# U^T x in column quarters and V in four 32-row tiles: a change to the last three batches of a fused linear-attention and mixer kernel

## The chip, the cores and the metric

The kernel runs on one core of a Trainium2 chip. The metric is the device time of one execution in microseconds. A core has five engines with queues of their own: PE (TensorE, matmuls), ACT (ScalarE), DVE (VectorE), POOL (GpSimd) and SP (SyncE, which here only issues DMAs). Each works through its queue in order; semaphores tie them together. Matmul results land in PSUM, which has eight banks of 512 fp32 columns, and ACT or DVE move them from there to the on-chip memory (SBUF).

## The reference

Four batches of 768 steps. Gated linear attention with 8 heads of 48 gives x (768 x 384 per batch), and a mixer follows: a low-rank mix over the sequence (rank 32) and an MLP over the channels.

```
for t in range(S):
    state = alpha[:, :, t, :, None] * state + einsum('bhd,bhe->bhde', k[:, :, t], v[:, :, t])
    y[:, :, t] = einsum('bhd,bhde->bhe', q[:, :, t], state)
x = y as (batch, 768, 384)
u = x + (x^T @ U @ V)^T          # U: 768 x 32, V: 32 x 768
out = u + relu(u @ w_ch1) @ w_ch2   # w_ch1: 384 x 1536, w_ch2: 1536 x 384
```

## The kernel before

The sequence of a batch is cut into six chunks of 128 steps. Each chunk goes through a chain: the logarithm of alpha (ACT), cumulative sums (PE), exponentials (ACT), scaling of k and q (POOL or DVE), transposes of both (PE and a copy, or in batch 3 one transposing DMA per chunk, line 588, called from `QUEUE_T`), scores (PE, line 604 or 435), masks (DVE), a state update, the output y (PE, lines 666 and 671 or 508 and 518) and a copy of it into `xb`, which is x in bf16. In ten of the 24 chunks (`PAIRS`: three chunk pairs of batch 0, two of batch 1) the work is laid out in another way, with pairs of steps; these use 64-row tiles of the PE array, and their rows are called even and odd parts in U and V (`ue_sb`, `ve_sb` in place of `u_sb`, `vm_sb`).

`stage_mix` then does the low-rank mix of one batch:

- U^T x (`f_utx`, line 686): six matmuls, one per chunk, each with 32 columns of U as the weights and all 384 columns of x moving. Chunk c writes to partitions 32 (c mod 4) onwards of one bank, so the four column groups of the array work side by side, and the four groups of 32 partitions hold four partial sums. ACT or DVE copies them to `utx` (128 x 384).
- V's part (line 716): for each chunk one matmul with 128 rows. `ve_sb` and `vm_sb` hold V four times below each other, so the product adds up the four partial sums. Each takes a bank, and a DVE addition (line 717) makes `ub`, which is u in bf16, from it and `xb`.
- The transposes of u to `uT`, in pairs of chunks: by PE (line 736) and a copy in batches 1 and 2, by a transposing DMA (line 722) in batch 3 (`QUEUE_U`). Batch 0 makes `uT` directly by matmuls (lines 705, 708).

`mlp1` (line 767, called a first-MLP group when its three matmuls stand together) makes one 128-row block of the hidden layer for half the sequence, and ACT (line 777) or DVE (line 779) take the relu. `mlp2` (line 793, three groups of four matmuls for each chunk, called second-MLP groups) and a DVE addition (line 799) make the output, which goes out by DMA (lines 802, 804).

The order of all work is not made by loops. `Plan.add` only lists each group of instructions with the engines that may run it; the listed dependencies decide which PSUM banks and buffers are bound together. `Plan.run` then goes through a text, `TABLE`, three characters for each group: two say which group, one says on which engine it runs (P, A, D, G, S). `SLOTS` names the bank or buffer for each new tile. So the place of a group in its engine's queue is the order of the text, and an engine never passes over a group that waits. The numbers beside the engines in `P.add` (`mm(...)`, 385, 460 and so on) are a planner's costs; nothing at run time reads them.

```
    def run(self, table, slots):
        nxt = iter(slots)
        for n in range(0, len(table), 3):
            ...
            op = self.ops[CODE.index(table[n]) * len(CODE) + CODE.index(table[n + 1])]
            for b in op.bufs:
                if b.slot is None:
                    b.slot = b.pool.slots[CODE.index(next(nxt))]
            op.fn({"P": "PE", "A": "ACT", "D": "DVE", "G": "POOL", "S": "SP"}[table[n + 2]])
```

Input tiles (alpha, k, q, v and the weights) and output tiles share a pool of 40 buffers; SP issues all DMAs, loads, stores and transposes, from one queue.

Of the kernel before, what the change touches and what calls it, by code (L numbers as in the profile page):

```python
# [16 lines left out]
A8SCcABASCzABQSETACePChACfAA+SCgACjDC1PC4AC3AC2AEVPEYABISA9SCiDCkPCmDClPBBSC5GEXADjADlPDnAEWACnDDmACoPCqDA-SCdGCrPCsDBDS  # L17
C0GDCPBCSC6GC7PBESCvPCpDC8PC+DDKACtPCuDCwPCxDDDDC9AC-PDADDBDABSAFGAGPAHDAJPAKADMPDPABKSCyDDEPDNADGPDFDDqGDsPBJSDpGDrPDtA
DuDDHPDJADZPBYSG2ABSSEaGBHSDLGDoAEcPDyPEeADIDBFSDQGDaPDbDDSPDUDDvPDwDBMSBLSDkGDzPD0DDxDG4PD8AD+PBRSEZGEbPEdDD3PDcPDdDDOA
BGSDRGDTPDVDG5AEAAD1PD2DBUSGfABOSEDGEfPEhDEgDD-AG7ABNSECGEBAG6ABTSBcSEUABPSD9GGhPGiAGjAGkAD4PELPBVSBWSGlGGmGBgSBXSGgGAAS  # L20
ADGBZSG8GAiSAjGAQSAeSAfGAgSAhGDWPDXDEiPD5PD7ABkSD6AEjPEkDEFPEEPEHAHNADYDEGDElPEMPENDAOSAPGARGEmPDfPAMSANGDePEnPEoADgPDiD
DhAAYSAZGBaSG9GAWSAUSAVGEIPEJDEKDHmAHPPHSAEPPGnPAXGASSATGHQABdSHTGBbSG3GEpAHRABiSBfSHOGAaSBhSBeSBoSAcSAkSBlSBjSAmSBpSAoS
BqSBmSGoPGqDGpDEOPAqSBnSHoPHrAEQPESDAuSAsSGuPGvDGwDEqPGrPGtDGsDERAErPHpAHqAHtGE8PE5PAwSAySEwPG+PHADE2PBrSEsAExPEyAE6PE7D
FFPE9PE+DA2SE3PEtPEzPFBPFCDFHPEuPFJPFGDE4AEvAE0PE1AF1PH-AFIDGyPF5PF3PF4DE-PFADFfPFgDF6AF2AFDPFhPFiAGxDFlPFmAFdPA4SACSFED
A0SFKDFLPFMAFNPFODG-PFjPFkAFeDA6SFVPFWAIBPICAFRPFSAHUGHBDHCPHDDAdGBsSGzPIEAIDAHFPFtPHGDHHDHIGIGGG0AAbAFuAHVPHXAG1AFnPHJP
B0SBwSBySB4SB8SFPPBuSBzSFQAHEDHKPHLAHMAHcPHdDHeDHsDIFAIVAFTPFUAFoAFrPFsAFpPHvPFqDHfDHxAHWPIXPIYAHuPHwDFvPFwDFZPFaDFzPF0D
HYAHiPHZPHbDHaDIZAAnAHyPHzDIHDFbPApAFcAHhPFxPFyAFXPHjPHkAHlAFYAHnGH1PH2DH3DH4DIIPIKAH6PAlGIaGIcPIbGIdPIfAIJPArGGTPIeAH7P
GNPH0DH8PH+AILDIMPH9DIODIgPIhDGBPIAGIPPH5GIRDF7PGZPHgGAzGAtAAvAAxAGOPINDITPF8PIQDIiDISGIWAIjPA5GGaPA3AGCPIUAAEGIkAIlPImD
GUPA1GA7AGbPGcDIvPIwDALGIzPI0DI1PI2DF9PF+DItPIuDGDPKLAGPPInPIpPIqDGEDKNPK0AI3PIxPIyDIoDKfAKOAI4AKPAKhPKjAKnGGVPGWDK2PK3A
LJAKlAJfPJgALeAKRAIrPIsDJRPJjPJSAJkDJdPJeAKiAKkAK6AKQAI5PJHPJIDJPPJQAJLPJMAI-PJAAK5AK4ALgPLkAJFPJGDJJPJKDLjABxSKmGKoPKqA  # L30
JTPJUDI6DKTGKVPJnPJoDLiALhABvSKMGBtSKSGKgAKUPJXPKWDKXDKbPKcDJlPLLPLMAJYDJbPJmAB9SB2SK8GKvPJBPK+PKwDKxDLAACASJcDJDPJEAB1S
KpPKrDGQDLOAK7GLNAJCAI9PI+ALPACESK9PK-DCMSNlAI7PI8DJVPJWALzAB3SK1GKsPKuDLBPLDDLCDKYPKZDJvPJNPJOAB6SLRGLTPLVAJhPL1PL2AL3A
B+SCCSB5SLHPLIANnPNqAB-SKtDLfALlGLnPKaDJwPL5GLQDCBSL4GLEPNrAKyPKzAJiAOIAB7SLKALpAGHPJZPGIPLSPLUAJaALFDLGGLmGKBPL6PL8DGJP
L7PGKDL9ALoPLqACNSCISCFSNoANsGLZPLaDJxPJyDNpACGSNtGKCPCKSCLSCQSCUSCDSLWPLXDL+PLrPKdPKeALYDLtDKDPJ7PLuPN2AN4PN5AJ8PJpPLbG
LsDLvDL-DLwGMADL0GOaAOcPOgAOfAOdACHSNmGN3GLcPN6ALdAN+GJ9PLxPLyDKEDMBPJqPNuSNvPNwDMCAMDPJrPOeAGMSNxDJ+DMEAN7AN8AOKPOMAAIG
MTPMUDMNPJ1PMLPMRPKGPMODJsDMMDCSSCRSOhGNyPNzDN0PMHPMIDKHPMFPMGDOsAOuPKIPMPPMQAMSDMJPMKDOOAMVPMWDKJDJ2PCWSOvAOLAMfPMXPMYD
J3PMjPM7POiGCYSO+AGFSCTSGGSPAPN1AONAObGGYSCJSCXSOtGCaSGSSKFSGLSN9GOwACPSOjSCVSOzGO0DOPDMkDMgDOxAOyAPBAPCAMbPMcDMpPMqAMlP
MmAJ4DNBPODPNDPMZPM-POEDMaAM8ANCACOSOQGNADM1PM2AOkPM5PNEDMxPMyAN-SM9PMhPM3PM4AJuSF-SMtPM6AMuAOJGOVPCZSPDGPEDOmDOlDOFDOWD
OXGMdPMeDM+AOnPOoDOpGNFPNGDMnPMoAMvPMiAOqPOrAOAPOBDO1SO2PO3DO4DOCDORSJ-SOSPOUDNHPMrPMsANRPMzPO5PO6DO7GOTDO8PO9ANSPGRSCbS
O-APFSJ5SPGPM0DPIDPHDGXSOGPOHANTPNUDOYPMwANIPPJPPKAOZAGASNJPNbPPLPNMPNcPPMAPPPPQDPSPPXPPNPPODPRSPYDPTDNdPNKDPUPPVDPWSNWP  # L40
# [45 lines left out]
class Plan:  # L86

    warm = None
# [36 lines left out]
    def run(self, table, slots):  # L128
        nxt = iter(slots)
        for n in range(0, len(table), 3):  # L130
            if table[n : n + 2] == "++":
                for _ in range(CODE.index(table[n + 2])):
                    self.warm()
                continue
            op = self.ops[CODE.index(table[n]) * len(CODE) + CODE.index(table[n + 1])]
            for b in op.bufs:
                if b.slot is None:
                    b.slot = b.pool.slots[CODE.index(next(nxt))]
            op.fn({"P": "PE", "A": "ACT", "D": "DVE", "G": "POOL", "S": "SP"}[table[n + 2]])

# [6 lines left out]
def kernel(  # L147
# [14 lines left out]
    C = 128  # L162
# [20 lines left out]
    QUEUE_U = (3,)  # L183
    P = Plan()
# [13 lines left out]
    filler = h1_s[1][:, 0, 0:512]  # L198
# [66 lines left out]
    bank.free[7] = 28000.0  # L265
    P.warm = lambda: nc.tensor.matmul(ps[:, 7, :], lhsT=filler[:, 0:128], rhs=filler, start=True, stop=True)

# [55 lines left out]
    def paired(b, c):  # L323
        return c // 2 < PAIRS[b]
# [355 lines left out]
    def stage_mix(b, xb, ub, uT):  # L680
# [10 lines left out]
        if b == 0:  # L691
            P.add({"PE": mm(DM)}, lambda e: f_utx(range(0, 4)), r=[x for c in range(4) for x in xk(b, xb, c)] + ["ue"], w=[xu], mode="C")
            P.add({"PE": mm(DM)}, lambda e: f_utx(range(4, NC)), r=[x for c in range(4, NC) for x in xk(b, xb, c)] + ["ue"], w=[xu], mode="C")
        else:
            P.add({"PE": mm(DM, DM)}, lambda e: f_utx(range(NC)), r=[x for c in range(NC) for x in xk(b, xb, c)] + ["ue" if paired(b, c) else "u" for c in range(NC)], w=[xu], mode="C")
        utx = Buf(utxs)
        P.add({"ACT": 385, "DVE": 460}, lambda e: copy(e, utx(), xu()[:, 0:DM]), r=[xu], w=[utx])
        if b == 0:
# [15 lines left out]
        for c in range(NC):  # L714
            hb = Buf(bank)
            P.add({"PE": mm(DM)}, lambda e, c=c, hb=hb: nc.tensor.matmul(hb()[:, 0:DM], lhsT=(ve_sb if paired(b, c) else vm_sb)[:, c * C : (c + 1) * C], rhs=utx(), start=True, stop=True), r=[utx, ("ve" if paired(b, c) else "vm", c // NT)], w=[hb])  # L716
            P.add({"DVE": 465}, lambda e, c=c, hb=hb: nc.vector.tensor_tensor(ub()[:, c, :], xb()[:, c, :], hb()[:, 0:DM], op=ALU.add), r=[hb] + xk(b, xb, c), w=[(ub, c)])  # L717
            if b in QUEUE_U:
                if c % 2 == 1:
                    P.add(  # L720
                        {"SP": 900.0},
                        lambda e, c=c: nc.sync.dma_start_transpose(
                            uT().rearrange("p j t -> p (j t)").rearrange("p (cj t) -> p cj t", t=C)[:, (c - 1) * NCT : (c + 1) * NCT, :],
                            ub()[:, c - 1 : c + 1, :].rearrange("t c d -> t (c d)"),
                        ),
                        r=[(ub, c - 1), (ub, c)], w=[(uT, "c", c // 2)], kind="U",
                    )
            elif c % 2 == 1 and b > 0:
# [10 lines left out]
                P.add({"PE": mm(*[C] * 6)}, f_tr, r=[(ub, c - 1), (ub, c)], w=[ub2])  # L739
# [14 lines left out]
    def mlp1(b, uT, h1, tt):  # L754
        for jt in range(NJ):
            hb = Buf(bank)

            if b == 0:
# [24 lines left out]
    def mlp2(b, ub, h1, c):  # L783
# [3 lines left out]
        for n, (lo, hi) in enumerate(parts):  # L787
# [11 lines left out]
            P.add({"DVE": 468}, lambda e, hb=hb, lo=lo, hi=hi: nc.vector.tensor_tensor(flat(ou)[:, lo:hi], ub()[:, c, lo:hi], hb()[:, 0 : hi - lo], op=ALU.add), r=[hb, (ub, c)], w=[(ou, n)])  # L799
# [58 lines left out]
```

## Time and profile before

| what | value |
|---|---|
| time, median of 3 runs | 160.99 us (160.51 to 161.96) |
| span of the profiled execution | 161.6 us |
| PE busy | 149.2 us, 92% |
| DVE, ACT, POOL busy | 105.7, 90.8, 66.0 us |
| granted TensorE clock | 1.000 |
| DMA | 31.05 MB, 192 GB/s mean, 81% of the engines' span |

The profile was taken in one execution; its span runs from the first to the last instruction, and the device time of that execution is not listed apart from the three runs. Busy time of an instruction includes its latency, so matmuls that follow each other overlap in it: their pace is read from the starts (the chain of waits lists stretches of PE by start and length), not from the mean duration. Rows of groups of instructions read: line, engine, operation, tiles written and read, shape, count, then busy time and mean duration in ns, then the idle time of the engine before them and what ended it.

### The profile page before, as it was taken

Reading aid. Unit: us, or ns where it says so; the run is one execution under the profiler, and the core shown is the slowest. Engines: PE = TensorE matmul, PEld = TensorE weight load, DVE = VectorE, ACT = ScalarE, POOL = GpSimd, SP = SyncE. Lnnn points to the kernel's source line nnn. Section 1 sums busy time; section 2 is a strip of 40 time slices with the busy share of each in tenths; the row PEclk is TensorE's granted clock in tenths of the full one; section 3 lists DMA queues with packets and bytes.
Section 4 is the critical chain, followed back from the end, with each engine's and each line's share of the span. In section 5 each row is a group of like instructions: output and inputs, shape, how many; then the busy total and the mean of one; then the engine's idle time right before and its main releaser. Section 6 shows DMA issues by size and latency. Waiting matters only on the chain.

```text
span 161.6 us, 4518 instructions
## 1 busy us (share of the span) xinstructions
PE 149.2 (92%) x1728; PEld 98.7 (61%) x1728; DVE 105.7 (65%) x232; ACT 90.8 (56%) x234; POOL 66.0 (41%) x104
## 2 busy tenths in 40 slices
PE   0699897999999999999999999999889999999992
PEld 0586675665667656666676666755457565666662
DVE  6269897966697729559975959682898172334143
ACT  4765797557977645996897472845524301445000
POOL 8099756477667340283563664144622000000000
PEclk9999999999999999999999999999999999999999
DMA  4999995999999969889999899999992047840034
GB/s 125 289 312 315 248 250 150 268 336 253 285 229 279 293 130 209 176 176 203 207 195 215 160 189 198 195 226 204 146 204 67 0 81 172 262 146 0 0 129 163
DMA packets 96964, 31.05 MB, mean 192 GB/s; under 512 B 90640, under 2 KB 96912, under 8 KB 96944
## 3 DMA queue, kind: packets, MB, share of 16 engines
q1 hardware_dynamic: 96944, 30.78, 81.2%
q8 instruction: 13, 0.21, 0.5%
q14 instruction: 7, 0.06, 0.1%
HBM read 23.89 MB, written 4.72 MB: 177 GB/s over the span
## 4 chain that ended last, share of the span: by engine, by line
PE 54%; SPq 20%; DMA 14%; issue 4%; POOL 3%; DVE 2%; ACT 1%; POOLq 0%; DVEq 0%
PE ps L793 24%; PE ps L767 19%; SPq L332 13%; DMA io<-in_q_dram 5%; SPq L339 3%; DMA kqt<-rkq 3%; DMA io<-in_moe_w_ch_dram 2%; DMA io<-in_k_dram 2%; DMA io<-in_v_dram 2%; PE ps L576 2%; SPq L802 2%; SPq L305 2%; PE ps L604 1%; PE ps L716 1%; DVE pm L614 1%
## 5 line engine op out<-in xcount | busy, mean ns | idle before, releaser
L767 PE MATMUL ps<-uT,w_sb 128*128 128x384 bf16 x288 | 53.2, 326 | 0.4 <-POOL w_sb L277 0.4
L793 PE MATMUL ps<-w_sb,h1t 128*128 128x384 bf16 (+2 forms) x300 | 53.1, 319 | 0.0
L777 ACT ACTIVATE h1t<-ps 128x384 bf16<-128x384 f32 x61 | 27.6, 497 | 23.2 <-PE ps L767 23.1
L793 PEld LDWEIGHTS <-h1t 128*128 128x128 bf16 x300 | 27.1, 97 | 15.6 <-issue 0.8
L767 PEld LDWEIGHTS <-w_sb 128*128 128x128 bf16 x288 | 26.5, 98 | 16.4 <-POOL w_sb L277 1.2
L779 DVE TENSOR_SCALAR h1t<-ps 128x384 bf16<-128x384 f32 x35 | 18.6, 553 | 14.2 <-PE ps L767 14.2
L799 DVE TENSOR_TENSOR io<-ub,ps 128x384 f32<-128x384 bf16 (+2 forms) x25 | 13.3, 533 | 10.2 <-PE ps L793 10.0
L614 DVE TENSOR_TENSOR pm<-ps,maskc 128x512 bf16<-128x512 f32 x28 | 17.7, 682 | 1.1 <-PE ps L604 1.1
L562 POOL TENSOR_TENSOR rkq<-io,ai 128x384 bf16<-128x384 f32 x12 | 11.4, 949 | 13.8 <-DMA io<-in_k_dram 8.5
L717 DVE TENSOR_TENSOR ub<-xb,ps 128x384 bf16<-128x384 bf16 x24 | 12.4, 548 | 4.5 <-PE ps L716 4.3
L446 DVE TENSOR_TENSOR pm<-ps,maskp 128x512 bf16<-128x512 f32 x20 | 13.1, 683 | 2.4 <-PE ps L435 2.4
L562 POOL TENSOR_TENSOR rkq<-io,aa 128x384 bf16<-128x384 f32 x11 | 10.0, 912 | 9.8 <-ACT aa L552 8.4
L273 ACT CAST xb<-ps 128x192 bf16<-128x192 f32 (+1 forms) x27 | 10.3, 404 | 6.3 <-PE ps L671 4.9
L277 POOL CAST rv<-io 128x384 bf16<-128x384 f32 x18 | 9.4, 529 | 10.3 <-DMA io<-in_v_dram 9.3
L277 POOL CAST w_sb<-io 128x384 bf16<-128x384 f32 x16 | 8.0, 518 | 7.5 <-DMA io<-in_moe_w_ch_dram 7.5
L273 ACT COPY kqt<-ps 128x512 bf16<-128x512 bf16 x17 | 9.8, 610 | 1.9 <-PE ps L576 1.2
L275 DVE COPY kqt<-ps 128x512 bf16<-128x512 bf16 x19 | 7.8, 420 | 4.0 <-PE ps L576 2.2
L551 ACT ACTIVATE ai<-ps 128x384 bf16<-128x384 f32 x14 | 6.9, 498 | 5.5 <-PE ps L543 3.6
L411 PE MATMUL ps<-ident,rkq 128*128 128x128 bf16 x80 | 8.2, 237 | 1.6 <-DVE rkq L393 1.0
L393 POOL TENSOR_TENSOR rkq<-io,ai 128x384 bf16<-128x384 f32 x8 | 7.3, 910 | 5.8 <-DMA io<-in_k_dram 5.8
L638 POOL TENSOR_TENSOR st<-sm,tot 128x384 bf16<-128x384 f32 x7 | 5.8, 829 | 6.6 <-DVE sm L654 6.6
L393 POOL TENSOR_TENSOR rkq<-io,aa 128x384 bf16<-128x384 f32 x9 | 8.2, 910 | 0.6 <-DMA io<-in_q_dram 0.3
(114 smaller groups left out, 217.1 us busy)
## 6 DMA issues: line engine op xcount, KB each, us to landing
io<-in_alpha_dram SPq DMA_DIRECT2D x24, 192.0 KB, 3.8
io<-in_q_dram SPq DMA_DIRECT2D x24, 192.0 KB, 3.7
io<-in_k_dram SPq DMA_DIRECT2D x24, 192.0 KB, 3.7
io<-in_v_dram SPq DMA_DIRECT2D x24, 192.0 KB, 3.8
io<-in_moe_w_ch_dram SPq DMA_DIRECT2D x24, 192.0 KB, 3.9
out_dram<-io SPq DMA_DIRECT2D x13, 192.0 KB, 1.9
out_dram<-io SPq DMA_DIRECT2D x20, 96.0 KB, 2.3
out_dram<-io SPq DMA_DIRECT2D x1, 120.0 KB, 1.7
```

What stands on the lines that cost most here:

```text
L273: nc.scalar.copy(dst, src)
L277: nc.gpsimd.tensor_copy(dst, src)
L332: lambda e: nc.sync.dma_start(t().rearrange("p (h j) d -> p h (j d)", j=2), src[b, hs, sl, :].rearrange("h (p j) d -> p h (j d)", j=2)),
L393: eng.tensor_tensor(jh(dst()[:, :, 0:D]), raw(a), jh(x()), op=ALU.mult)
L446: nc.vector.tensor_tensor(dst, s2, maskp.to_broadcast([C, 2, 2, C]), op=ALU.mult)
L562: eng.tensor_tensor(dst()[:, :, 0:D], a(), x(), op=ALU.mult)
L614: nc.vector.tensor_tensor(pm()[:, :, par, :], s2, maskc.to_broadcast([C, HP, C]), op=ALU.mult)
L767: nc.tensor.matmul(hb()[:, 0:TW], lhsT=w1_sb[:, ct, jt * 128 : (jt + 1) * 128], rhs=u_half(uT, ct, tt, b in QUEUE_U), start=(ct == 0), sto ...
L777: nc.scalar.activation(dst, hb()[:, 0:TW], AF.Relu)
L779: nc.vector.tensor_scalar_max(dst, hb()[:, 0:TW], 0.0)
L793: nc.tensor.matmul(hb()[:, 0 : hi - lo], lhsT=h1()[:, jt, c * C : (c + 1) * C], rhs=w2_sb[:, jt, lo:hi], start=(jt == 0), stop=(jt == NJ - 1),
L799: P.add({"DVE": 468}, lambda e, hb=hb, lo=lo, hi=hi: nc.vector.tensor_tensor(flat(ou)[:, lo:hi], ub()[:, c, lo:hi], hb()[:, 0 : hi - lo], ...
```

## The change

For batches 1 to 3 (batch 0 keeps the old way, `SUM_U`):

- U^T x (`f_utq`): each chunk's x is cut into four column quarters of 96, and quarter g goes to column group g. A group now sums all six chunks itself, so 24 matmuls of 96 columns take the place of six of 384, and the bank holds whole sums: 32 partitions for each quarter, 96 columns wide. `utx` is copied with 96 columns instead of 384.
- V's part (`f_q`): two groups per batch, one for each half of the sequence (three chunks). Each has 12 matmuls of 96 columns with 32 rows: row group g multiplies V by quarter g of `utx` and writes to its own bank, three chunks side by side (288 columns). A group takes four banks at once. Six matmuls of 384 columns are left out for these 24.
- The additions that make `ub`: eight of 128 x 288 (half h, quarter g) in place of six of 128 x 384. A pair of chunks can be transposed when all four quarters of its half (for the middle pair, of both halves) are there (`quarters`).
- `TABLE` and `SLOTS` are new throughout. Counted by engine the texts hold, before and after: PE 373 and 361 groups, ACT 233 and 218, DVE 209 and 241, POOL 89 and 78, SP 167 and 167. DMAs are the same in number and size, in another order.
- A filler matmul for an idle PE (`warm`) gets another form; neither text calls for it.

```
+    SUM_U = (0,)
+    NG, W = 4, DM // 4
+    quarters = lambda ub, cs: [(ub, h, g) for h in sorted({c // NT for c in cs}) for g in range(NG)]
...
+        rows = lambda g: slice(32 * g, 32 * g + R)
+
+        def f_utq(cs):
+            for c in cs:
+                for g in range(NG):
+                    nc.tensor.matmul(
+                        xu()[rows(g), 0:W], lhsT=(ue_sb if paired(b, c) else u_sb)[:, c, :], rhs=xb()[:, c, g * W : (g + 1) * W],
+                        start=(c == 0), stop=(c == NC - 1), skip_group_check=True,
+                    )
...
-            P.add({"PE": mm(DM, DM)}, lambda e: f_utx(range(NC)), ...)
+            P.add({"PE": mm(*[W] * NC)}, lambda e: f_utq(range(NC)), ...)
         utx = Buf(utxs)
-        P.add({"ACT": 385, "DVE": 460}, lambda e: copy(e, utx(), xu()[:, 0:DM]), r=[xu], w=[utx])
+        wide = DM if b in SUM_U else W
+        P.add({"ACT": 385, "DVE": 460}, lambda e: copy(e, utx()[:, 0:wide], xu()[:, 0:wide]), r=[xu], w=[utx])
+        if b not in SUM_U:
+            for h in range(2):
+                qb = [Buf(bank) for _ in range(NG)]
+                cs = range(h * NT, (h + 1) * NT)
+
+                def f_q(e, cs=cs, qb=qb):
+                    for n, c in enumerate(cs):
+                        for g in range(NG):
+                            nc.tensor.matmul(
+                                qb[g]()[:, n * W : (n + 1) * W], lhsT=(ve_sb if paired(b, c) else vm_sb)[rows(g), c * C : (c + 1) * C], rhs=utx()[rows(g), 0:W],
+                                start=(n == 0), stop=(n == NT - 1), skip_group_check=True,
+                            )
+
+                P.add({"PE": mm(*[W] * NT)}, f_q, ..., w=qb, mode="L")
+                for g in range(NG):
+
+                    def f_u(e, h=h, g=g, qb=qb):
+                        v = lambda t: t()[:, h * NT : (h + 1) * NT, g * W : (g + 1) * W]
+                        nc.vector.tensor_tensor(v(ub), v(xb), qb[g]()[:, 0 : NT * W].rearrange("p (c d) -> p c d", c=NT), op=ALU.add)
+
+                    P.add({"DVE": 370}, f_u, ..., w=[(ub, h, g)])
...
-                        r=[(ub, c - 1), (ub, c)], w=[(uT, "c", c // 2)], kind="U",
+                        r=quarters(ub, (c - 1, c)), w=[(uT, "c", c // 2)], kind="U",
...
-                P.add({"PE": mm(*[C] * 6)}, f_tr, r=[(ub, c - 1), (ub, c)], w=[ub2])
+                P.add({"PE": mm(*[C] * 6)}, f_tr, r=quarters(ub, (c - 1, c)), w=[ub2])
```

More of the change, by code (lines that the diff above doesn't have):

```diff
@@ L197 @@
     h1_s = slots("h1t", 2, [128, NJ, S], BF16)
-    filler = h1_s[1][:, 0, 0:512]
+    filler = h1_s[1][:, 0, 0:256]
     nc.vector.memset(filler, 0.0)
@@ L264 @@
     bank = Pool([ps[:, i, :] for i in range(8)])
-    bank.free[7] = 28000.0
-    P.warm = lambda: nc.tensor.matmul(ps[:, 7, :], lhsT=filler[:, 0:128], rhs=filler, start=True, stop=True)
+    P.bank = bank
+    P.warm = lambda x: nc.tensor.matmul(x[:, 0:256], lhsT=filler[:, 0:128], rhs=filler, start=True, stop=True)
     def bf(x):
```

117 lines of the change are left out of this document (66 added, 51 removed).

## The prediction

> **What bounds the kernel now.** I read the page first: its busy times and its slices.
>
> ```profile
> span 161.6 us, 4518 instructions
> PE 149.2 (92%) x1728; PEld 98.7 (61%) x1728; DVE 105.7 (65%) x232; ACT 90.8 (56%) x234; POOL 66.0 (41%) x104
> PE   0699897999999999999999999999889999999992
> DMA  4999995999999969889999899999992047840034
> ```
>
> PE (TensorE) is at nine tenths in nearly every slice; the DMA engines are full too, but only until about 120 us. So the share alone does not name the bound, and I cut the span at the U^T x steps of the four batches, as the timeline dates them: 58.27, 95.59 and 126.46 us begin those of batches 1, 2 and 3.
>
> ```profile
> 31.40:58.27 26.87, 26.20 (x350) 16.76 (x347) 18.95 (x41) 19.30 (x49) 17.07 (x29) 1.00 1.00 269
> 58.27:95.59 37.32, 37.25 (x416) 25.16 (x416) 27.35 (x52) 28.17 (x73) 18.06 (x25) 1.00 0.97 191
> 95.59:126.46 30.87, 29.57 (x301) 18.57 (x297) 22.96 (x43) 14.93 (x38) 11.13 (x14) 1.00 0.89 171
> 126.46:158.80 32.34, 32.17 (x213) 19.84 (x212) 12.96 (x26) 7.35 (x17) 0.00 (x0) 1.00 0.36 107
> ```
>
> After the stretch come its length and the busy time of PE, weight loads, VectorE (DVE), ScalarE (ACT) and GpSimd (POOL). From 58 us on PE idles 0.07, 1.30 and 0.17 us. A microsecond less of PE work there is a microsecond off the end, if the other queues deliver as much earlier. The chain of waits shows where they hardly do:
>
> ```profile
> 82.58 0.17 PE ps L666 x4
> 82.75 0.20 PE ps L671 x8
> ...
> 88.40 0.37 PE ps L604 x8
> ...
> 114.06 4.30 DMA kqt<-rkq
> 118.41 0.40 PE ps L604 x8
> ...
> 126.53 0.43 PE ps L686 x6
> ...
> 128.37 0.65 PE ps L716 x4
> 129.02 0.65 PE ps L793 x4
> 129.67 0.16 PE ps L716
> ...
> 131.78 0.16 PE ps L716
> ...
> 135.20 11.70 PE ps L767 x72
> 146.90 11.74 PE ps L793 x84
> 158.73 0.30 DVE io L799
> ```
>
> At 118.41 the scores of batch 3 (L604) start when a transpose by DMA lands; from there to 158.73 there is only PE. The steps that change are L686 (U^T x) and L716 (V's part).
>
> **The change, part by part.** *U^T x.* Now six matmuls of 384 columns in four column groups take two rounds. A round of 384 columns costs 0.65/4 = 0.1625 us (128.37 row), so two are 0.325, and the other 0.105 of the 0.43 is the change of the array's tiling in and out. The scores say the same: eight of 128 columns in two groups are four rounds of 0.056 = 0.22, and 0.37 is shown. New: 24 matmuls of 96 columns in four column groups, six rounds. A round of 96 columns costs 0.17/4 = 0.0425 (82.58 row): 0.255 + 0.105 = 0.36. It saves 0.07 us.
>
> *V's part.* Now 0.65 + 0.16 + 0.16 = 0.975 us for six. New: two halves of 12 matmuls of 96 columns, in four 32-row tiles; three rounds are 0.13, with the switch 0.23, two halves 0.465. It saves 0.51.
>
> No row shows four row tiles of 32. The nearest ones are 64-row tiles and the 48x64 quadrants:
>
> ```profile
> 39.08 0.35 PE ps L435 x16
> ...
> 51.91 0.30 PE ps L518 x16
> ```
>
> L518, two row tiles of 48 columns, runs 16 in 0.30 with its switch, 18.75 ns each: 12 would be 0.225. L435 runs four quadrants at once, 16 of 128 columns in 0.35 and not in 16 x 0.056 = 0.89. I take 0.23. Bounds: with no switch at all both parts would cost 0.51 and save 0.90 a batch; with row tiles that don't overlap a half would cost 12 x 0.0425 + 0.105 = 0.615, V 1.23, and the batch would lose 0.19 after U's 0.07.
>
> The Trainium skill's page "TensorE: Matmul & The Clock Gate" (Part 3, Measured speedup vs the span model) gives 3.07 times, not four, for four row tiles of 32 rows and 512 columns. By that, as an estimate, a half is 12 x 0.0425/3.07 + 0.105 = 0.27 and the three batches save 0.24 us less; no row here can tell the two apart.
>
> So a batch saves 0.07 + 0.51 = 0.58 us of PE, three save **1.74 us** (bounds: -2.7 to +0.6).
>
> *Evictions.* These are the rows that price them:
>
> ```profile
> L717 DVE TENSOR_TENSOR ub<-xb,ps 128x384 bf16<-128x384 bf16 x24 | 12.4, 548 | 4.5 <-PE ps L716 4.3
> L799 DVE TENSOR_TENSOR io<-ub,ps 128x384 f32<-128x384 bf16 x23 | 12.5, 549 | 9.9 <-PE ps L793 9.8
> L799 DVE TENSOR_TENSOR io<-ub,ps 128x240 f32<-128x240 bf16 x1 | 0.4, 405 | 0.2 <-PE ps L793 0.2
> L273 ACT CAST utx<-ps 128x384 bf16<-128x384 f32 x3 | 1.4, 478 | 2.3 <-PE ps L686 2.3
> L273 ACT CAST xb<-ps 128x192 bf16<-128x192 f32 x14 | 4.2, 332 | 1.3 <-PE ps L518 1.2
> L273 ACT CAST xb<-ps 128x384 bf16<-128x384 f32 x13 | 6.2, 482 | 4.9 <-PE ps L671 4.9
> ```
>
> utx shrinks from 384 to 96 columns: on ACT 150 ns for 192 columns is 0.78 a column, so about 257 in place of 478 ns; 0.22 us of latency, hidden behind second-MLP groups. The adds go from six of 548 ns to eight of 288 columns; 405 to 549 ns over 144 columns is 1.0 a column, so 453 ns each: 3.62 in place of 3.29 us, +0.33 a batch on DVE, which is not on the path while PE has filler. But each add now holds a quarter of three chunks, so the first transposed pair waits for four adds and not two, and the second pair for all eight.
>
> In batch 3 that matters most, since behind it there is no other work. The new order leaves 13 second-MLP groups of batch 2 between U^T x and the first MLP group (11 now): 13 x 0.65 + 0.36 + 0.465 = 9.3 us of cover. Under it: U^T x 0.36, eviction 0.26 and the first half behind one filler group, so the first add starts near 1.4; eight adds that stand together in DVE's order end near 5.1.
>
> ```profile
> L722 SPq DMA_TRANSPOSE uT<-ub x3: 1212/1230/1259, 129.6 to 133.4; - x3
> DMA to landing us min/median/max: 2.7/2.8/2.8
> ```
>
> The second transpose is issued near 5.1 and lands near 7.9, 1.4 us ahead of need; the third (+1.2) is needed only by a later group. I cost the longer wait at nothing. Without the cover each microsecond would be one on the end.
>
> *The order.* Though called little moved, it gives other engines work: DVE has 241 groups in place of 209, ACT 218 for 233, POOL 78 for 89. DVE gets 11 more relu evictions, 7 more x evictions, 3 state scalings, 5 scalings of q and k, 2 more q/k copies; less one utx and one V copy:
>
> ```profile
> L779 DVE TENSOR_SCALAR h1t<-ps 128x384 bf16<-128x384 f32 x35 | 18.6, 553 | 14.2 <-PE ps L767 14.2
> L275 DVE CAST xb<-ps 128x384 bf16<-128x384 f32 x1 | 0.6, 557 | 1.3 <-PE ps L671 1.3
> L275 DVE COPY kqt<-ps 128x512 bf16<-128x512 bf16 x19 | 7.8, 420 | 4.0 <-PE ps L576 2.2 <-PE ps L411 1.8
> L562 DVE TENSOR_TENSOR rkq<-io,aa 128x384 bf16<-128x384 f32 x3 | 1.9, 621 | 3.0 <-DMA kqt<-rkq 2.3 <-DMA io<-in_q_dram 0.6 <-ACT aa L552 0.2
> ```
>
> That is 11 x 0.553 + 7 x 0.557 + 3 x 0.55 + 5 x 0.62 + 2 x 0.42 - 1.1 + 1.0 (adds) = 15 us at full durations, so DVE stands near 120 of 160. The first weights keep their place (37th in SP's queue in both), so I move nothing at the start.
>
> U^T x of batch 3 has two second-MLP groups fewer ahead of it (1.3 us) and the savings of batches 1 and 2 (1.16): it would start at 126.46 - 2.46 = 124.0, and the end follows 32.27 + 1.3 - 0.58 = 33.0 us later, at 157.0 instead of 158.73. For this the scores of chunks 5 and 2 must start at 119.6: between them and it stand their own 2 x 0.33, four second-MLP groups (2.6) and three output groups of 0.17 + 0.20, 4.4 us in all. Now the last transpose of keys and queries is issued at 117.80:
>
> ```profile
> 110.35 1.17 SPq L802 DMA_DIRECT2D out_dram<-io  x2
> 115.44 1.56 SPq L802 DMA_DIRECT2D out_dram<-io  x2
> 117.80 1.82 SPq L588 DMA_TRANSPOSE kqt<-rkq  x1
> kqt<-rkq SPq DMA_TRANSPOSE x6, 3.8
> ```
>
> With 3.8 us to landing that is 121.6, 2.0 too late. In the new order it is 134th, not 140th, in SP's queue, with 5 output stores ahead of it, not 11; at 0.6 to 0.8 us a store that is some 4 us earlier, 117.6. So it is in time by 2 us, less what the q load ahead of it waits for.
>
> **Sum.** The profiled span of 161.6 lies within the runs (160.51 to 161.96) and what lies around it is not shown, so I take the difference to the median: 160.99 - 1.74 = 159.25, said as **159.3 us**.
>
> **Rivals.**
> - *The saving and the waits of 113 to 118.* The 1.2 us that PE idles there goes too, since the stores have moved behind: 159.25 - 1.2 = 158.1. For it: the full DMA engines until 120 us. Against: a new order has waits of its own.
> - *The saving is eaten.* The last transpose still lands at 121.6: PE waits 2.0 us for it, which takes the 1.74 and 0.3 more: 161.2. For it: the q load of the last chunk now stands right ahead of it. Against: fewer stores do.
> - *DVE becomes the bound (slower).* Between U^T x of batches 1 and 2 its 53 groups, 30.3 us at full durations, show as 27.35 busy; the new order puts 64 groups there, 35.6 us, so some 32.1 busy against 36.7 of PE (37.3 less the batch's 0.6). DVE idled 10.0 us there in order, for others. If 5 remain, 37.1, nothing is lost; it decides slower from 8 on, and with 8.6 (40.7 us, 4 us over PE) the time is 159.25 + 4.0 = 163.2. For it: one queue in order, evictions that hold PE's banks, and V taking four banks at a time. Against: DVE's waits are mostly for PE itself, the longest of this stage for U^T x, and those shrink when DVE is late:
>
> ```profile
> DVE utx L275 <- PE ps L686: 3.3, 1, 3.3
> ```
>
> - *The row tiles don't overlap.* V 1.23: +0.19 a batch, 161.6. Against: L435.
>
> The Trainium skill's page "TensorEngine Tiling (Array Packing)" (Performance Considerations, PSUM Bottleneck) says that tiling makes TensorE faster but not the emptying of PSUM, which may then bind; that is the DVE rival, and the 0.33 us more adds beside 0.58 less PE are its sign here.
>
> **How the numbers follow.** Forecast 0.40 (own range 158.5 to 160.2, half of it over 1% faster); waits gone too 0.18; eaten 0.14; no overlap 0.03; DVE 0.25. About 1%, 1.6 us, is what a measurement of this kernel tells from no change. Faster: 0.20 + 0.18 = 0.38; slower: 0.25, and 0.03 of the eaten case, transposes over 1.4 us later than now, = 0.28; within 1%: 0.34. The range leaves out a tenth on each side: 157.6 to 163.6.
>
> **What would show it.** Right: 24 matmuls of U^T x in about 0.36 us, 12 of V in 0.23, 24 adds of about 450 ns, U^T x of batch 3 near 124.0 and PE without a gap from it to the end. Wrong: V at 0.6 a half; a wait of the scores for a transpose of over 1 us near 119; PE waiting in 58 to 95 us for evictions by DVE with DVE over 32 busy.

## The result and the profile after

The changed kernel takes 160.15 us in the median (158.81 to 161.06); the kernel before, run beside it, takes 161.69 us (159.87 to 164.28). The ratio of the two is **0.9942 [0.9914, 0.9969]** (in brackets its 95% interval): 0.6%, or 0.9 us, faster. Medians here are over all executions, but ratios, and the differences between two kernels on one chip, leave out executions more than 1.5% above the fastest of their kernel, so they are not quotients and differences of the medians. The forecast was 1.7 us faster.

From the page of the changed kernel, the lines that answer to those of before:

```profile
span 157.9 us, 4730 instructions
...
PE 147.7 (94%) x1836; PEld 98.7 (63%) x1836; DVE 118.6 (75%) x264; ACT 83.6 (53%) x219; POOL 58.6 (37%) x93
...
PE   0499999999999999999999999999999999999992
...
DMA  5999999999999999999799998996860073406662
```

The 8 that PE showed twice near 113 to 121 us is gone. DVE carries 13 us more (15 were counted at full durations). The device times of the executions lie some 1.75 us above their spans (the one profiled here: 159.65 and 157.9). So the profile of before, with a span of 161.6 us, belongs to an execution of about 163.4 us, 1.7 us above the median, and the 3.7 us between the two spans overstate what the change does.

The same stretches, cut at the U^T x steps of batches 1, 2 and 3 (58.49, 95.56 and 121.95 us). Length, then busy time of PE, weight loads, DVE, ACT and POOL; the last three numbers are the granted clock, the share of the DMA engines and GB/s:

```profile
31.40:58.49 27.09, 26.94 (x369) 17.18 (x371) 24.45 (x54) 17.88 (x46) 15.52 (x26) 1.00 1.01 260
58.49:95.56 37.07, 36.88 (x456) 25.15 (x460) 31.78 (x64) 24.83 (x67) 15.69 (x20) 1.00 1.02 200
95.56:121.95 26.39, 26.38 (x333) 17.62 (x336) 24.11 (x48) 12.81 (x33) 8.47 (x12) 1.00 0.73 143
121.95:155.10 33.15, 33.05 (x256) 20.30 (x256) 15.92 (x35) 5.08 (x12) 0.00 (x0) 1.00 0.43 125
```

I shall call them stretch 1-2, 2-3 and 3-end, the last one measured to the start of the last addition. Before: 37.39, 30.87 and 32.20 us. (The prediction has 37.32 and 32.27: it took 58.27 us from the chain of waits but 95.59 and 126.46 from the timeline, which dates these steps 0.07 us earlier.) After: 37.07, 26.39 and 33.08. The work of two second-MLP groups (1.3 us) has moved from 2-3 to 3-end. With those counted back, 3.2 of the 3.9 us between the two profiles are in 2-3, which holds the changed steps of batch 2 alone.

The end of the chain of waits of the changed kernel (start, length, what):

```profile
121.30 0.65 PE ps L841 x4
121.95 0.37 PE ps L711 x24
122.32 0.76 PE ps L841 x4
123.08 0.24 PE ps L732 x12
123.31 1.41 PE ps L841 x8
124.72 0.24 PE ps L732 x12
124.96 6.61 PE ps L841 x40
131.57 10.24 PE ps L815 x63
...
155.03 0.30 DVE io L847
```

U^T x (L711) takes 0.37 us where 0.36 was predicted, a half of V (L732) 0.24 where 0.23 was. But look at the second-MLP groups between them. Four matmuls of L841 take 0.65 us at 121.30 and 0.76 behind U^T x; eight take 1.41 behind a half of V, and forty take 6.61 instead of ten times 0.65. **Each tiled group costs 0.11 us once more, in the group behind it.** The chain of before had it as well, in a row that the prediction left out, behind its U^T x, against the eight matmuls just ahead of it:

```profile
125.23 1.30 PE ps L793 x8
...
126.97 1.41 PE ps L793 x8
```

So by these rows of batch 3 a batch costs 0.37 + 0.11 + 2 x (0.24 + 0.11) = 1.18 us now, and 0.43 + 0.11 + 0.975 = 1.52 before. It saves 0.34, not 0.58.

The other steps: the group of the additions, by form, and then the timeline (start, length) at an eviction of utx and in SP's queue:

```profile
L742 DVE TENSOR_TENSOR ub<-xb,ps 128x288 bf16<-128x288 bf16 x24 | 9.3, 449 | 2.7 <-PE ps L732 2.5
```

```profile
122.37 0.24 ACT L288 CAST utx<-ps 128x96 bf16<-128x96 f32 x1 [0.16 <-PE ps L711]
...
113.91 1.24 SPq L603 DMA_TRANSPOSE kqt<-rkq  x1
```

An addition takes 449 ns (453 predicted), the eviction of utx 0.24 us (0.257), and the last transpose of keys and queries is issued at 113.91, 3.9 us earlier than before (4 predicted).

### The profile page after: what moved, and what is told of

It is laid out like the page before. It is cut to its first block, busy times and chain, and to the rows that moved or that the text cites. A ratio compares the mean times of both kernels' runs of the same rounds, so it can differ in the third digit from the quotient of the medians.

```text
span 157.9 us, 4730 instructions
## 1 busy us (share of the span) xinstructions
PE 147.7 (94%) x1836; PEld 98.7 (63%) x1836; DVE 118.6 (75%) x264; ACT 83.6 (53%) x219; POOL 58.6 (37%) x93
## 4 chain that ended last, share of the span: by engine, by line
PE 72%; SPq 14%; DMA 5%; DVE 3%; issue 2%; ACT 1%
PE ps L815 29%; PE ps L841 28%; SPq L347 11%; DMA io<-in_alpha_dram 5%; PE ps L619 2%; PE ps L686 1%; PE ps L556 1%; PE ps L591 1%; PE ps L784 1%; PE ps L681 1%; DVE rkq L577 1%; SPq L295 1%; SPq L320 1%; PE ps L642 1%; PE ps L732 1%
## 5 line engine op out<-in xcount | busy, mean ns | idle before, releaser
L841 PE MATMUL ps<-w_sb,h1t 128*128 128x384 bf16 (+2 forms) x300 | 52.8, 320 | 0.0
L815 PE MATMUL ps<-uT,w_sb 128*128 128x384 bf16 x288 | 52.0, 326 | 0.0
L825 ACT ACTIVATE h1t<-ps 128x384 bf16<-128x384 f32 x50 | 23.1, 499 | 28.8 <-PE ps L815 28.7
L841 PEld LDWEIGHTS <-h1t 128*128 128x128 bf16 x300 | 26.8, 97 | 15.0
L827 DVE TENSOR_SCALAR h1t<-ps 128x384 bf16<-128x384 f32 x46 | 24.1, 552 | 12.9 <-PE ps L815 12.2
L577 POOL TENSOR_TENSOR rkq<-io,aa 128x384 bf16<-128x384 f32 x9 | 8.2, 915 | 19.6 <-PE ps L815 10.3
L577 POOL TENSOR_TENSOR rkq<-io,ai 128x384 bf16<-128x384 f32 x11 | 10.0, 916 | 6.0 <-DMA io<-in_k_dram 4.7
L288 ACT CAST xb<-ps 128x192 bf16<-128x192 f32 (+1 forms) x20 | 7.2, 374 | 9.0 <-PE ps L686 7.0
L742 DVE TENSOR_TENSOR ub<-xb,ps 128x288 bf16<-128x288 bf16 x24 | 9.3, 449 | 2.7 <-PE ps L732 2.5
L288 ACT COPY kqt<-ps 128x512 bf16<-128x512 bf16 x15 | 8.7, 597 | 1.7 <-PE ps L426 0.7
L549 ACT ACTIVATE lt<-io 128x384 bf16<-128x384 f32 x14 | 7.1, 524 | 2.8 <-issue 2.8
L567 ACT ACTIVATE aa<-ps 128x384 bf16<-128x384 f32 x14 | 6.8, 495 | 3.3 <-PE ps L558 1.7
L408 POOL TENSOR_TENSOR rkq<-io,aa 128x384 bf16<-128x384 f32 x8 | 7.2, 910 | 3.4 <-ACT aa L401 3.2
```

The source lines that it names most:

```text
L288: nc.scalar.copy(dst, src)
L577: eng.tensor_tensor(dst()[:, :, 0:D], a(), x(), op=ALU.mult)
L742: nc.vector.tensor_tensor(v(ub), v(xb), qb[g]()[:, 0 : NT * W].rearrange("p (c d) -> p c d", c=NT), op=ALU.add)
L815: nc.tensor.matmul(hb()[:, 0:TW], lhsT=w1_sb[:, ct, jt * 128 : (jt + 1) * 128], rhs=u_half(uT, ct, tt, b in QUEUE_U), start=(ct == 0), sto ...
L825: nc.scalar.activation(dst, hb()[:, 0:TW], AF.Relu)
L827: nc.vector.tensor_scalar_max(dst, hb()[:, 0:TW], 0.0)
```

## The experiments

Four theories had to be told apart. *The steps*: less PE work shortens the time. *The order*: what came is the gain of the new order, above all of the output stores that no longer stand ahead of batch 3's loads. *The cover*: the longer wait for four quarters is free only in this order. *The leaks*: the saving is made, and something takes it back.

### The spread: both kernels again

No edit; the two kernels as they are.

> The kernel before, unchanged, for a second profile. The profile on which the prediction rests has a span of 161.6 us, and a run takes 1.75 us more than its span, so that execution was near 163.4 us, above the usual 160 to 162. Theory 1 (the order before loses time in some executions to late transposes of batch 3): a span of 158.5 to 160 with no wait of the scores for a transposing DMA, and U^T x of batch 3 at 124 to 125 us. Theory 2 (the waits belong to every execution and the rest varies): the waits near 113 to 118 us, 1.2 us in all, again, and U^T x of batch 3 after 125.5. Time ratio 0.995 to 1.005 by both.

> The changed kernel, unchanged, for a second profile and the noise of the ratio. Ratio 0.990 to 0.997 by all theories; span 157.5 to 159.5, U^T x of batch 3 at 122 to 123.5 us.

Before: 163.81 us, ratio 0.9983 [0.993, 1.0035]. Its profile, of an execution of 164.44 us, has stretches of 37.21, 31.96 and 32.20 us, so 2-3 is long again, and theory 2 holds. Its longest wait of PE there:

```profile
PE ps L666 <- POOL st L638: 1.9, 1, 1.9
```

The chain leads back from this wait to a load of keys, which SP issues at 111.60 us, right behind output stores.

After: 161.91 us, 0.9893 [0.9813, 0.9972]. After on a second chip:

> The changed kernel again, beside the one with the old steps in the new order, to part the two. If the saved PE work reaches the end: 0.5 to 1.7 us less than that kernel (the stretches from U^T x of batch 1 to the last matmul were 96.6 and 97.7 us, 1.06 apart, in the first profiles). If it does not: within 0.4 us of it.

161.7 us, 0.987 [0.9755, 0.9985]. All three profiles of the changed kernel have stretches of 37.07 or 37.08, 26.38 or 26.39 and 33.08 or 33.09 us, but U^T x of batch 1 starts at 58.49, 60.18 and 60.01. From 58 us on these three repeat each other to 0.01 us; what varies lies ahead, where SP issues loads one behind the other without a pause. So the stretches tell differences that the medians cannot.

### One half of the change at a time

The new steps in the order of before: V's halves stand where the first and the fourth or fifth of its six matmuls stood, the additions where they were.

```
-  PE: V.0 m2 V.1 ... V.5          DVE: u.0 ... u.5
+  PE: V.half  m2 ... V.half       DVE: u.h0g0 ... u.h1g3 at the old places
```

> Only the steps change: U^T x in quarters and V in row tiles, with the order and the engines of before (V's two groups at the places of the first and the fourth or fifth of its six matmuls, the adds at those of the old adds). If the saved PE work makes the gain (theory A, 0.58 us a batch): 1.0 to 1.7 us less than before, ratio 0.990 to 0.994. If the new order makes it (theory B): ratio 0.998 to 1.003, as waits for the quarters eat what PE saves.

170.87 us, ratio **1.0468 [1.0407, 1.053]**, which neither theory expected. Its longest waits of PE behind U^T x of batch 1 (us in total, times, the longest), and a row of its chain:

```profile
PE ps L815 <- ACT tot L569: 1.4, 1, 1.4
PE ps L732 <- DVE ub L742: 1.4, 6, 0.6
PE ps L732 <- DVE io L847: 0.8, 2, 0.5
PE ps L841 <- DVE ub L742: 0.6, 1, 0.6
```

```profile
135.19 7.04 PE ps L841 x32
```

V now asks for four banks at once, and PE waits for the additions that free them (L732 for L742, six times). Behind the last of these waits the granted clock is 0.50 from 135.4 to 138.8 us, and 32 matmuls that take 5.2 us at the usual pace take 7.04. So some 1.7 of the 7 us are the clock's, but two executions at a mean clock of 1.000 took 169.64 and 170.69 us as well. At these places of the old order the longer wait and the four banks are not free; in the new order they are.

The old steps in the new order (three matmuls of V at the place of each half, three additions at the places of four):

```
-  PE: V.half0 ... V.half1         DVE: u.h0g0 u.h0g1 u.h0g2 u.h0g3
+  PE: V.0 V.1 V.2 ... V.3 V.4 V.5 DVE: u.0 u.1 u.2
```

> Only the order and the engines change: the old six matmuls of U^T x, V's six and the six adds of 384 columns, in the places that the new order gives to their halves. Theory A (saved PE work): ratio 1.000 to 1.004, no gain, since PE has 1.7 us more than the changed kernel. Theory B (the order): ratio 0.993 to 0.997, the same as the changed kernel or nearly.

> The old six matmuls and six adds in the new order, again. Saved PE work counts: ratio 0.994 to 0.998 to before, U^T x of batch 1 to that of batch 2 near 37.1 us, to batch 3 near 27.1, from there to the last matmul near 33.5. Order alone makes the gain: ratio 0.989 to 0.993, like the changed kernel.

161.42 us, ratio **0.9904 [0.9861, 0.9946]**, and on the second chip 161.38 us, 0.9893 [0.9819, 0.9967]: as much as the whole change. The stretches of the second one:

```profile
58.55:95.65 37.10, 37.10 (x416) 25.44 (x418) 31.23 (x62) 24.92 (x67) 14.40 (x19) 1.00 0.99 194
95.65:122.73 27.08, 26.81 (x292) 17.76 (x294) 24.00 (x46) 13.03 (x33) 9.66 (x13) 1.00 0.80 151
```

Stretch 1-2 is 37.10 us here and 37.07 with the new steps: of batch 1's saving nothing shows. Stretch 2-3 is 0.69 us longer, 3-end 33.43 and so 0.35 longer. In 2-3 PE idles 0.27 us, because here the large eviction of utx is not covered; this is the waits' one row:

```profile
PE ps L716 <- ACT utx L273: 0.3, 1, 0.3
```

So 0.69 is the batch's 0.34, the 0.27 of this wait, and 0.08 that no row names.

### The output stores

The kernel before with eleven output stores moved in SP's queue behind batch 3's last transpose of u. Nothing else is touched.

```
-  SP: load store store load transpose store ... transpose
+  SP: load load transpose ... transpose(u) store store store ...
```

> The kernel before, with nothing changed but the place of 11 output stores in the SP queue: behind the last transposing DMA of batch 3's u, not among the last loads. If the order's gain comes from loads that no longer stand behind stores (batch 2 to batch 3 took 30.9 and 32.0 us before, 26.4 in the changed kernel, with 1.3 us of work moved behind): this stretch shortens by 1 to 2.5 us, ratio 0.985 to 0.994. If the loads are bound by the DMA engines or by free buffers: unchanged, 0.997 to 1.003.

161.58 us, ratio **0.9885 [0.9833, 0.9937]**, as on the same chip the old steps in the new order (0.9893) and the changed kernel (0.987). Its stretch 2-3, and then SP's timeline at the last transpose of keys and queries:

```profile
95.64:124.31 28.67, 28.67 (x301) 18.54 (x297) 22.55 (x43) 15.12 (x39) 10.15 (x14) 1.00 0.73 140
```

```profile
115.75 1.24 SPq L588 DMA_TRANSPOSE kqt<-rkq  x1
117.04 1.88 SPq L802 DMA_DIRECT2D out_dram<-io  x3
```

28.67 us instead of 30.87, PE without a gap, and the transpose 2.05 us earlier than at 117.80. The other stretches change little (37.16 and 32.20). One queue's order, with not a matmul changed, gives what the change gives.

### Is PE the bound? More of V

Each half of V worked out three times; the last one counts.

```
-  for n, c in enumerate(cs):
+  for n, c in list(enumerate(cs)) * 3:
```

> The changed kernel, in which each half of V's part is worked out three times over (36 matmuls of 96 columns instead of 12, the last 12 count): 24 more matmuls at the pace measured (0.24 us less 0.105 for 12) are 0.27 us a half, 0.54 us of PE a batch, 1.6 us in all. Theory 1, PE sets the pace everywhere: stretches 37.61, 26.93 and 33.62 us, time +1.6 us (1.0%). Theory 2, between U^T x of batches 1 and 2 another queue sets the pace and PE waits 0.43 us for it at the scores near 89 us: stretches 37.2, 26.9 and 33.6 us, that wait gone, time +1.2 us. Theory 3, loads set the pace up to 110 us: 37.1, 26.4 and 33.6 us, time +0.6 us.

162.69 us, ratio 0.9997 [0.9946, 1.0047], 1.9 us above the changed kernel on the same chip. The first two stretches:

```profile
59.43:97.01 37.58, 37.39 (x505) 25.66 (x508) 31.78 (x64) 24.82 (x67) 13.76 (x18) 1.00 0.99 186
97.01:124.45 27.44, 26.95 (x380) 18.12 (x384) 24.20 (x48) 12.81 (x33) 10.42 (x13) 1.00 0.83 155
```

Stretch 1-2 grows by 0.51 us and 3-end by 0.52 (33.60): 48 more matmuls of 96 columns in four row tiles take 0.51 us, 10.6 ns each, a quarter of 42.5. Theory 1 holds where loads do not bind. Stretch 2-3 grows by 1.05: 0.5 of PE work and 0.5 of a wait for a transpose of keys, so there the loads bind as well. The three sum to 2.1 us, near the 1.9 of the times. And it makes the riddle of 1-2 sharper: added PE work shows whole there, saved work not at all.

### The cover in batch 3

Six of the 13 second-MLP groups between U^T x of batch 3 and the first first-MLP group stand behind nine first-MLP groups.

```
-  PE: UTx(3) m2 V m2 m2 V m2 x10            m1 x9 ...
+  PE: UTx(3) m2 V m2 m2 V m2 x4             m1 x9  m2 x6 ...
```

> The changed kernel with six of the 13 second-MLP groups that stand between U^T x of batch 3 and the first first-MLP group moved behind nine first-MLP groups; all other work keeps its place. The first-MLP groups then stand 3.9 us earlier, 5.7 us after U^T x of batch 3. Theory 1, as predicted, the longer wait for four quarters costs nothing only because of this cover: the second transpose lands some 7.5 us after U^T x, PE waits about 1.8 us there, the last stretch is 33.08 + 1.8 = 34.9 us, time +1.8 us (1.1%). Theory 2, the cover is far more than needed (transposes land by 5.7 us): last stretch 33.1 us, no difference in time.

164.25 us, ratio **1.005 [1.0005, 1.0094]**, 3.5 us above the changed kernel beside it. Its chain, and then its longest wait of PE:

```profile
124.60 0.37 PE ps L711 x24
...
127.67 1.54 DVE ub L742 x4
129.21 0.03 DVE io L847
129.24 2.79 DMA uT<-ub
132.03 0.14 issue
132.16 4.55 PE ps L815 x27
```

```profile
PE ps L815 <- DMA uT<-ub: 1.8, 1, 1.8
```

The transposed u lands 7.4 us after U^T x and PE waits 1.8 us, both as expected. The time grew by more than that. 0.5 us is in 3-end too (35.41 in place of 33.08, less 1.8). In the changed kernel the first-MLP group starts 9.6 us after U^T x (131.57 less 121.95), so its cover has 2.2 us to spare. The stretches ahead of the edit are 0.7 and 1.1 us longer in this profile (37.76 and 27.47): a load of values lands late, and DVE loses another turn of the kind that the next experiments show (a state addition of 1.30 us at 83.56). Why this variant meets them is not shown.

### What takes batch 1's saving: VectorE and GpSimd

A first try: one copy of transposed keys ahead of one output addition on DVE, since the chain of 87 to 89 us leads over it.

```
-  DVE: io(L847)  xb  sm  io(L847)  kqt copy
+  DVE: io(L847)  xb  sm  kqt copy  io(L847)
```

> The changed kernel with one DVE instruction moved: the copy of the keys of batch 2's chunk 5 ahead of one output addition. In the changed kernel the scores wait 0.43 us for this copy near 89 us, and the stretch from U^T x of batch 1 to that of batch 2 is 37.07 us, no shorter than with the old steps (37.09). If DVE's order there swallowed the saving: 36.6 to 36.8 us, and 0.3 to 0.4 us less in all. If the loads set the pace there: 37.07 again.

161.55 us, 0.9887 [0.9798, 0.9977]; stretch 1-2 36.96 us, 0.11 shorter, 2-3 27.27. That is less than the 0.3 to 0.5 us expected of this cause; the copy's place is not the main one.

Then I compared the lengths of single instructions between the changed kernel and the old steps in the same order. One stands out: DVE's state addition (L653, L638 in the old lines) with both inputs in SBUF. From the timelines, the changed kernel first, then the old steps:

```profile
85.49 1.25 DVE L653 TENSOR_TENSOR st<-sm,tot 128x384 bf16<-128x384 f32 x1
...
85.41 0.91 POOL L577 TENSOR_TENSOR rkq<-io,aa 128x384 bf16<-128x384 f32 x1
```

```profile
85.89 0.67 DVE L638 TENSOR_TENSOR st<-sm,tot 128x384 bf16<-128x384 f32 x1
...
86.11 1.23 POOL L562 TENSOR_TENSOR rkq<-io,aa 128x384 bf16<-128x384 f32 x1
```

The two take turns. In the changed kernel GpSimd starts 0.08 us first and DVE takes 1.25 us; with the old steps DVE is 0.22 us first, takes 0.67, and GpSimd 1.23 in place of 0.91. In five profiles of the changed kernel DVE loses, in three of the old steps it wins. If that is the cause, moving only the moment of DVE's addition must turn it, both ways.

```
-  PE: transposes of keys (batch 2, chunk 3), state update, output step     [changed kernel]
+  PE: state update, transposes of keys, output step
-  PE: transposes of keys, state update, output step of chunk 2             [old steps, new order]
+  PE: transposes of keys, output step of chunk 2, state update
```

> The changed kernel with one group moved on PE: the state update of chunk 3 of batch 2 stands ahead of the transposes of the same chunk's keys, so it starts 0.22 us earlier. In four profiles of the changed kernel the state addition behind it (VectorE, line 653, both inputs in SBUF) starts 0.08 us after a scaling on GpSimd (line 577) and takes 1.25 us; in three profiles of the old steps in this order it starts 0.2 us before that scaling and takes 0.67, and the scaling takes 1.23 and not 0.91. Theory 1, the two take turns and the later one waits, which costs VectorE 0.58 us and brings the 0.43 us wait at the scores: here the addition takes some 0.7 us, the scaling 1.2, stretch 1 to 2 is 36.5 to 36.6 us and not 37.07, and if the next stretches stay at 26.39 and 33.08 the time falls by 0.5 us, 0.3%. Theory 2, the long addition is not what PE waits for: the addition is short and the stretch stays at 37.0 to 37.1. A gain that loads take back shows as a longer stretch 2 to 3, up to 26.9.

> The converse: the kernel before with its steps in the order of the changed kernel, the same state update moved on PE behind the output step of chunk 2, 0.37 us later. The state addition on VectorE would then start some 0.17 us after the scaling on GpSimd, not 0.2 us before it. Theory 1: the addition takes 1.1 to 1.25 us and not 0.67, VectorE is 0.9 us later from there on, PE waits for it at the scores and stretch 1 to 2 is 37.5 to 38.0 us, not 37.09. Theory 2: the addition takes 0.55 to 0.67 us and the stretch stays under 37.3.

The changed kernel with the state update ahead, its timeline and then its stretches:

```profile
86.63 0.60 DVE L653 TENSOR_TENSOR st<-sm,tot 128x384 bf16<-128x384 f32 x1
...
86.78 1.23 POOL L577 TENSOR_TENSOR rkq<-io,aa 128x384 bf16<-128x384 f32 x1
```

```profile
59.86:96.63 36.77, 36.77 (x456) 25.20 (x460) 31.45 (x64) 24.89 (x67) 14.01 (x18) 1.00 0.98 192
96.63:124.96 28.33, 27.15 (x332) 17.43 (x336) 24.32 (x48) 12.80 (x33) 9.73 (x13) 1.00 0.85 153
```

The old steps with the state update later, in the same two views:

```profile
88.28 1.02 DVE L638 TENSOR_TENSOR st<-sm,tot 128x384 bf16<-128x384 f32 x1
...
87.98 0.91 POOL L562 TENSOR_TENSOR rkq<-io,aa 128x384 bf16<-128x384 f32 x1
```

```profile
60.39:98.13 37.74, 37.39 (x416) 25.43 (x418) 31.86 (x62) 24.95 (x67) 13.77 (x18) 1.00 0.97 188
```

Both turn as theory 1 said: the addition falls to 0.60 us and stretch 1-2 to 36.77, and here the addition rises to 1.02 and the stretch to 37.74. With the collision out of the way the new steps are 0.33 us shorter than the old ones (37.10), which is the batch's 0.34. That this collision eats the saving of batch 1 is shown, by one profile each way. The gain of 0.30 us was less than the 0.5 expected, since the batch saves less than I had counted.

As a version it brings nothing. Beside it ran the changed kernel again:

> The changed kernel again, to compare the moved state update with on one chip: stretches 37.07, 26.39 and 33.08 us, the long state addition of 1.25 us; time 0.3% over the kernel with the state update moved by theory 1 of that run, equal by its theory 2.

That took 161.32 us, ratio 0.9891 [0.9833, 0.9949]; with the state update ahead it is 162.03 us, 0.9919 [0.9885, 0.9952]. Its stretch 2-3 is 28.33 us in the profile, 1.9 longer, for a late load of keys and its transpose. The old steps with the update later: 162.72 us, 0.9955 [0.9914, 0.9997].

### The start, and the steps in the median

> The changed kernel again, beside its order with the old steps on the same chip. In the profiles so far the three stretches from U^T x of batch 1 to the last addition are 37.07, 26.39 and 33.08 us, 1.06 us shorter together than with the old steps in this order (37.09, 27.08, 33.43). Theory 1, the late start of three profiles (60.0 to 60.2 us and not 58.5) is chance of the loads: start in the median as with the old steps, this kernel 1.06 us, 0.65%, faster than that one. Theory 2, the changed kernel itself starts later: the same stretches, but a time equal to the old steps' or up to 0.5 us longer, as on the two chips before.

> The kernel before with all its steps, in the order of the changed kernel, beside that kernel. Stretches 37.09, 27.08 and 33.43 us by both theories. Theory 1: start as the changed kernel's, time 1.06 us longer than its. Theory 2: start some 1.4 us earlier in the median, time equal or up to 0.5 us shorter.

After: 161.63 us, 0.9818 [0.9747, 0.989]. Old steps in the new order: 161.07 us, 0.9821 [0.9768, 0.9875]. On that second chip, measured once more, the two again cannot be told apart, though the stretches of the new steps are 1.06 us shorter (0.65%). One guess was that a longer program starts later. Small matmuls ahead of each of V's make the program longer:

```
-  matmul(hb[:, 0:DM], V[c], utx)
+  for n in (4,) * 6 + (DM,): matmul(hb[:, 0:n], V[c], utx[:, 0:n])
```

> The kernel before with its steps in the order of the changed kernel; ahead of each of V's 18 matmuls of batches 1 to 3 stand six more of four columns into the same bank, which the true one overwrites, so it has 108 more matmuls and weight loads, as many as the changed kernel. All that runs before U^T x of batch 1 is the same. In seven profiles with the new steps U^T x of batch 1 starts at 58.5 to 60.2 us (median 59.5), in six with the old ones at 58.0 to 58.6 (median 58.5). Theory 1, a longer program starts later: U^T x of batch 1 at 59.2 us or later. Theory 2, it is not the length: 58.6 or earlier. The 108 matmuls cost some 0.3 to 0.5 us of PE in each later stretch by both.

164.65 us, 1.0072 [1.0035, 1.0108]. U^T x of batch 1 starts at 59.76 us, but that says nothing of the program's length. The edit reaches batch 0 as well: of its 144 small matmuls 36 stand ahead of this U^T x (the expectation counted 108, all behind it), some 0.9 us of PE at the price below. The short program with the state update later, whose work up to there is untouched, starts at 60.39, and the changed kernel at 57.89 in its fifth profile. In five profiles of the changed kernel the start lies between 57.89 and 60.18 (mean 59.2), in four with the old steps in the new order between 57.95 and 60.39 (mean 58.9). The length of the program is not shown to matter; the start varies with the loads of the first 30 us. Each of the three stretches grew by 0.89 to 0.91 us for 36 matmuls of four columns, 25 ns each.

The new order also meets a lower clock less often. The mean granted clock of an execution is 0.990 or less in 44 of 103 executions of the kernel before on these three chips, and in none of 22 of the changed kernel and 24 of the old steps in the new order. That is not the whole gain: among the executions above it, the changed kernel is 1.3 to 2.2 us faster in the mean.

**What stays open:** why the 1.06 us of the stretches is not in the medians. A hint, not a proof: with the old steps 2-3 is 27.08 us in all four profiles that leave it as it is; with the new ones 26.38 to 26.66 in five and 27.27 to 28.33 in the four variants, each time with a wait for a load or a transpose. The new steps seem to have used up the lead of batch 3's loads.

## Why the prediction was right or wrong

The direction came out as forecast, but by luck: what the times show, another cause brings too. Two steps of the prediction failed. The saving of a batch was mis-sized: 0.58 us, where 0.34 was measured. And the sum "160.99 - 1.74 = 159.25" gave the whole gain to PE's steps and put the new order at nothing, though the order alone, with the old steps, gives what the change gives (ratios 0.9904, 0.9893 and 0.9821).

- **U^T x, V, additions, evictions: right.** 0.37, 0.24, 449 ns, 0.24 us against 0.36, 0.23, 453 ns, 0.257. Four row tiles overlap. By the Trainium skill's page "TensorE: Matmul & The Clock Gate" (Part 3, Measured speedup vs the span model) the estimate for a half, from 3.07 times, was 0.27; the trace's 0.24 and the 10.6 ns of each added matmul, four times as fast as 42.5, say full overlap.
- **The saving of a batch: mis-sized.** The step that failed is "the other 0.105 of the 0.43 is the change of the array's tiling in and out". Out is another 0.11, in the group behind; V's halves add two such changes a batch where V had none. 0.34 instead of 0.58, 1.0 us in all instead of 1.74. The rows of before could have told it: 1.41 against 1.30 for eight matmuls. That the stretches differ by 1.06 us in all is not three times 0.34: it is 0.03, 0.69 and 0.35.
- **"A microsecond less of PE work there is a microsecond off the end": wrong for batch 1.** The collision of DVE with GpSimd near 86 us takes its 0.3 us. The prediction saw DVE's busy time rightly (31.78 against 32.1) and asked whether it would be too much; it did not ask what DVE's instructions meet on another engine. The Trainium skill's page "SBUF — State Buffer" (Who interferes with whom) has the rule: an instruction of VectorE with two SBUF inputs and one of GpSimd that reads SBUF exclude each other, and whoever is first decides who blocks. The trace agrees: the addition takes 1.25 us where GpSimd is 0.08 us ahead, and 0.67 where VectorE is 0.22 us ahead.
- **The smaller eviction: its gain was left out.** It was costed as hidden latency. In the new order it is not: the large one makes PE wait 0.27 us in batch 2.
- **The longer wait costs nothing: right, and for the reason given.** Slack 2.2 us (1.4 predicted); with 3.9 us of cover away PE waits 1.8. At their places in the old order the new steps lose 4.7%.
- **The order: the rival "The saving and the waits of 113 to 118" names what the profile shows**, and it was held at 0.18; its time of 158.1 us did not come (160.15). The profile of before that it rests on was no usual execution: the prediction set its span of 161.6 us beside device times, where it belongs to 163.4. Stores among loads cost the profiled execution of before 2.2 us in stretch 2-3, not the 1.2 us of PE's idle time in that place. The argument against the rival, that a new order has waits of its own, was right as to the collision, but that is smaller.
- **The median.** The forecast put PE's saving alone on the median. What the times show, 0.9 us in the first measurement and 1.1 to 1.8% in the later ones, is met by the old steps in the new order, and on one chip by moving the stores alone. In the profile U^T x of batch 3 begins at 121.95 us, where PE's saving was to bring it to 124.0.
- **The other rivals.** "Eaten" by the last transpose: no, it is issued 3.9 us earlier and PE does not wait. DVE as the bound at 163.2 us: no, PE idles 0.19 us in that stretch. Row tiles that do not overlap: no.

## What to carry to other kernels

Before costing a change of PE work, undo it in thought: ask what the new order alone does, above all which stores stand ahead of which loads in a shared queue, since here that alone gave as much as the whole change. Price a change of the array's tiling at both ends, by the group behind it as well as by the tiled group. Where a saving vanishes, compare the lengths of single instructions in two traces of the same order: one that is twice as long names the collision.

## What the hardware showed unexpectedly

- A group in row or column tiles costs 0.105 us within itself and 0.11 us in the full-array group behind it (0.76 against 0.65 us for four matmuls, 1.41 against 1.30 for eight).
- A VectorE addition with both inputs in SBUF takes 0.55 us alone (at another place of the same trace) and 1.25 behind a GpSimd scaling that starts 0.08 us earlier; the scaling takes 0.91 alone and 1.23 behind the addition.
- A matmul of four columns with its own weights costs 25 ns of PE (0.9 us for 36), more than twice one of 96 columns in four row tiles (10.6 ns).
- The new steps in the old order met a granted clock of 0.50 for 3.4 us, right behind 3 us in which PE waited again and again. One such stretch, as an estimate, lowers the mean clock of an execution of 169 us to 0.990 and costs it 1.7 us. Most of the executions of before with a lower clock show 0.987 to 0.990, but no profile caught the moment there.
